# One more token chunk with the seven block products in the second FFN layer, and a new written-out order

## The chip, the cores and the metric

The kernel runs on one core of a Trainium2 chip. The time is device microseconds of one execution, the median of several. The profile is one further execution, recorded by the hardware profiler; its times count from its first instruction.

## The reference

For 8 batches of 576 positions with 8 heads of 64 the reference computes causal attention over a window of 64 positions, puts the heads side by side to a row of 512, takes a two-dimensional FFT of every batch (positions and features), keeps the real part, adds it to the input (`u`), normalises every row, and runs a feed-forward network on it:

```python
un = (u - mu) / np.sqrt(var + 1e-06)
ch = np.maximum(un @ w_ch1, 0.0) @ w_ch2      # 512 -> 2048 -> 512
return (u + ch).astype(np.float32)
```

## The kernel before, in words

**Work and tiles.** The 4608 rows are 36 tiles of 128 rows (`T`), worked on in attention, and 18 chunks of 256 rows (`c`), worked on in the FFN. A tile of attention is: loads of k, q and v (line 538), a split of k and q into two float16 parts and a DMA transpose of them (593), scores on TensorE (662), masking on VectorE (677), the exponential on ScalarE (685), a split of the result and two DMA transposes (715), the product with v (739), and normalising (758). Tiles 0 to 10 use float32 and TensorE transposes instead. When tiles 4 and 8 of a pair of batches are there, the FFT of a batch follows (1023, 1061), then for each tile a gather from DRAM, statistics and a split and transpose into the FFN's input (1135 to 1221).

**FFN.** TensorE works with three float16 products for each float32 product (`PASSES`). In `ffn` (chunks 1 to `SEVEN`-1; chunk 0 is float32) the first layer has 16 blocks of 12 matmuls with 256 columns (1419), ReLU into two parts on ScalarE (1428) and VectorE (1431), and the second layer has 16 blocks of 6 matmuls with 512 columns (1400). In `ffn7` (chunks from `SEVEN` on) the first layer is the same (1573); the second takes 8 steps `j`, each with seven block products of three matmuls with 256 columns (1548), as in Strassen's scheme, and so needs more work ahead of it: ReLU (1584), four sums of 128x128 (1589), the high part (510 or 506) and the low part (1597), on VectorE, ScalarE or GpSimd. The last chunk takes its last step by plain products (1560). The seven products also need sums of w2's blocks. `weight_sums` makes these once (VectorE lines 1493 to 1511, eight sets), into buffers that belong to attention until its last tile is done with them, so they can be made only at the end of attention and have to be there for the first `ffn7` chunk. Six chunks (12 to 17) use `ffn7`.

**Order.** Every step is an operation, entered by `plan.op` in a fixed sequence of calls and numbered in that sequence. `ORDER` lists these numbers: each engine works off its own in the order in which they stand there, so TensorE, VectorE, ScalarE, GpSimd and SyncE (which issues nearly all transfers) are five queues in order. `SECOND` holds the operations that go to the second of the two engines allowed to them. `plan.follow` checks the table and works out gaps, which serve for the warm-up matmuls (1759) in the first microseconds only; no time of it enters the program elsewhere. The tables were written by a planner that is not part of the kernel.

The numbers of `ORDER` can be turned back into operations by counting the calls for a given `SEVEN`; what the section on the change says of the two tables was read so.

Of the kernel before, what the change touches and what calls it, by code (L numbers as in the profile page):

```python
# [58 lines left out]
SEVEN = 12  # L59
# [339 lines left out]
def attn_fft_ffn_kernel(ctx: ExitStack, tc: tile.TileContext, q, k, v, w1, w2, gidx, dft_d, dft_s, mask, out):  # L399
# [1311 lines left out]
    for T in range(NTT):  # L1711
# [6 lines left out]
        if n in (4, 8):  # L1718
            base += FFT_AT + (FFT1 if T == 8 else 0)
            fft(2 * pb + n // 8, base)  # L1720
            for i, m in enumerate(range(0, 4) if n == 4 else range(4, 9)):
                args = NT * pb + m, base + NORM_AT + i + (EARLY if T == 4 and i > 1 else 0)
                if args[0] // 2 >= SEVEN + 4:
                    behind.setdefault(args[0] // 2, []).append(args)
# [66 lines left out]
```

## Time and profile before

| | us |
|---|---|
| median of 3 runs (lowest, highest) | 942.36 (940.58, 946.78) |
| the profiled execution: its own time | 945.16 |
| its span, first to last instruction | 943.4 |

The page of the profile gives the busy time of each engine, and then the span in 40 slices. PE is TensorE's matmuls, PEld its weight loads, DVE VectorE, ACT ScalarE, POOL GpSimd, SP SyncE. The end of a matmul is modelled, so that PE can be called busy where it does not work at its peak; the step from one block's start to the next one's is the safer reading.

### The profile page before, as it was taken

How to read it: one execution, taken by the hardware profiler on the slowest of the kernel's cores; microseconds unless marked ns; L12 is line 12 of the kernel's file. 1: busy time of each engine (PE TensorE's matmuls, PEld its weight loads, DVE VectorE, ACT ScalarE, POOL GpSimd, SP SyncE). 2: the span in 40 equal slices, each digit the busy share in tenths (PEclk: the TensorE clock that was granted, in tenths of full speed). 3: DMA queues.
4: the chain of work that ended last, by engine and by line, in shares of the span. 5: the costliest groups of instructions: out<-in, count | busy, mean ns of one | idle time of the engine just before them, and what ended most of it. 6: DMA issues, size and time to landing. Idle time of an engine off the chain costs nothing.

```text
span 943.4 us, 24809 instructions
## 1 busy us (share of the span) xinstructions
PE 924.2 (98%) x9717; PEld 703.2 (75%) x9717; DVE 705.3 (75%) x1982; ACT 435.1 (46%) x979; POOL 441.5 (47%) x823
## 2 busy tenths in 40 slices
PE   7799999999999999999999999999999999999998
PEld 6677777666766676666766676667779998888887
DVE  5898998887767866677658757888898965675664
ACT  6875777834555424445443543444334442422111
POOL 2653464744744555465746544655601454124012
PEclk9999999999999999999999999999999999999999
DMA  9997447999689969879979788785402032210100
GB/s 231 239 263 202 133 144 147 167 173 169 136 193 163 198 122 167 185 152 207 197 168 190 150 162 169 163 147 108 137 12 57 24 96 65 68 35 13 57 24 23
DMA packets 300230, 128.69 MB, mean 136 GB/s; under 512 B 277768, under 2 KB 278152, under 8 KB 300112
## 3 DMA queue, kind: packets, MB, share of 16 engines
q1 hardware_dynamic: 297248, 118.06, 59.6%
q0 software_dynamic: 2720, 8.92, 3.3%
q8 instruction: 76, 1.25, 0.6%
q14 instruction: 42, 0.34, 0.1%
q10 hardware_dynamic: 144, 0.13, 0.0%
HBM read 60.76 MB, written 19.94 MB: 86 GB/s over the span
## 4 chain that ended last, share of the span: by engine, by line
PE 83%; DMA 5%; DVE 4%; POOL 3%; SPq 2%; issue 2%; ACT 1%; POOLq 0%; DVEq 0%; ACTq 0%
PE ph L1419 22%; PE po L1400 22%; PE ph L1573 13%; PE po L1548 11%; PE pz L1061 3%; PE pg L1023 3%; PE pa L739 3%; PE psc L662 2%; DMA kn<-in_k 1%; POOL flex L516 1%; DMA ve<-va 1%; DMA qn<-in_q 1%; DMA pt<-flex 1%; SPq L1277 1%; PE py L850 1%
## 5 line engine op out<-in xcount | busy, mean ns | idle before, releaser
L1400 PE MATMUL po<-ws,hh 128*128 128x512 f16 (+1 forms) x1116 | 284.5, 391 | 0.5 <-issue 0.2
L1419 PE MATMUL ph<-room,ws 128*128 128x256 f16 x2112 | 256.1, 273 | 1.8 <-DVE hh L1431 1.8
L1419 PEld LDWEIGHTS <-ws 128*128 128x128 f16 x2112 | 205.3, 98 | 54.1 <-issue 2.8
L1400 PEld LDWEIGHTS <-hh 128*128 128x128 f16 x1056 | 101.1, 98 | 90.0 <-DVE hh L1431 0.7
L1573 PE MATMUL ph<-room,ws 128*128 128x256 f16 x1152 | 136.2, 273 | 0.0
L1573 PEld LDWEIGHTS <-ws 128*128 128x128 f16 x1152 | 112.6, 98 | 13.6
L1428 ACT ACTIVATE hh<-ph 128x512 f16<-128x512 f32 x88 | 52.3, 594 | 120.8 <-PE ph L1419 99.8
L685 ACT ACTIVATE pr<-pr,nm 128x128 f32<-128x128 f32 x288 | 91.2, 393 | 31.5 <-DVE nm L677 31.4
L1431 DVE SCALAR_TENSOR_TENSOR hh<-ph,hh 128x512 f16<-128x512 f32 x88 | 60.4, 686 | 36.6 <-ACT hh L1428 36.5
L1135 POOL DMA_INDIRECT mt<-md,gix x34 | 42.0, 1235 | 96.7 <-DVE mv L1163 81.5
L677 DVE CUSTOM_DVE_ANT_0 pr<-psc,mskb 128x128 f32<-128x128 f32 x288 | 65.0, 287 | 25.9 <-PE psc L662 19.7
L1584 ACT ACTIVATE hx<-ph 128x512 f32<-128x512 f32 x47 | 27.8, 595 | 113.3 <-PE ph L1573 103.7
L1589 DVE TENSOR_TENSOR hx<-hx 128x128 f32<-128x128 f32 x164 | 45.1, 318 | 37.8 <-ACT hx L1584 36.2
L1548 PEld LDWEIGHTS <-hh 128*128 128x128 f16 x658 | 64.4, 98 | 7.6
L1597 POOL TENSOR_TENSOR hl<-hx,hh 128x256 f16<-128x256 f32 (+1 forms) x40 | 28.0, 730 | 77.3 <-DVE hh L510 53.7
L516 POOL TENSOR_TENSOR up<-un,up 128x128 f16<-128x128 f32 x84 | 40.9, 516 | 46.3 <-ACT up L506 38.8
L516 POOL TENSOR_TENSOR flex<-pr,flex 128x128 f16<-128x128 f32 x92 | 42.5, 494 | 36.2 <-ACT flex L506 18.2
L1548 PE MATMUL po<-ws,hh 128*128 128x256 f16 x282 | 51.2, 273 | 0.0
L1597 DVE TENSOR_TENSOR hl<-hx,hh 128x896 f16<-128x896 f32 x37 | 40.4, 1097 | 7.8 <-ACT hh L506 6.5
L752 POOL TENSOR_TENSOR rc<-rc,mone 128x4 f32<-128x4 f32 x29 | 32.5, 1129 | 26.6 <-DVE rc L747 16.8
L739 PE MATMUL pa<-ve,pt 128*64 128x65 f16 (+1 forms) x776 | 37.0, 203 | 2.5 <-ACT ve L506 1.8
L1548 PE MATMUL po<-ws,hl 128*128 128x256 f16 x141 | 38.4, 273 | 0.0
(244 smaller groups left out, 1718.6 us busy)
## 6 DMA issues: line engine op xcount, KB each, us to landing
room<-in_moe_w_ch SPq DMA_DIRECT2D x20, 512.0 KB
flex<-in_moe_w_ch SPq DMA_DIRECT2D x12, 512.0 KB
ve<-va SPq DMA_DIRECT2D x47, 130.0 KB
flex<-in_v SPq DMA_DIRECT2D x22, 256.0 KB
xs<-xu SPq DMA_DIRECT2D x22, 256.0 KB
xv<-xs SPq DMA_DIRECT2D x22, 256.0 KB
out<-xv SPq DMA_DIRECT2D x21, 256.0 KB
md<-mp SPq DMA_DIRECT2D x24, 192.0 KB
```

Source lines behind the costliest of these rows:

```text
L516: eng.tensor_tensor(out=out[:, k : k + w], in0=in0[:, k : k + w], in1=in1[:, k : k + w], op=al)
L677: nc.vector.tensor_tensor_reduce(out=t["pr", g][:, hp], in0=t["ps", g][:, hp], in1=mskb[:, m : m + P], scale=-0.125, scalar=3.0e38, op0=AL ...
L685: nc.scalar.activation(pr, pr, AF.Exp, bias=t["nm", g][:, hp : hp + 1], scale=-1.0)
L739: nc.tensor.matmul(pa[sl, hp], pt[:, sl], v_, start=(x == 0), stop=(x == len(mm) - 1))
L1400: nc.tensor.matmul(t["po"][i], l_, r_, start=(f == 0 and x == 0), stop=(f == NKF - 1 and x == len(mm) - 1))
L1419: nc.tensor.matmul(ph, l_, r_, start=(x == 0), stop=(x == len(mm) - 1))
L1428: nc.scalar.activation(t["hh", j][:, 0], ph, AF.Relu)
L1431: nc.vector.scalar_tensor_tensor(out=hh[:, 1], in0=ph, scalar=0.0, in1=hh[:, 0], op0=ALU.max, op1=ALU.subtract)
L1548: nc.tensor.matmul(t["po", bk][:, x], t["h", j][a][:, slot], right(n, j, b_), start=(j == 0 and k == 0 and n in opens), stop=(j == seven - ...
L1573: nc.tensor.matmul(ph, l_, r_, start=(x == 0), stop=(x == len(mm) - 1))
L1589: eng.tensor_tensor(out=x[:, o], in0=x[:, p0], in1=x[:, p1], op=al)
L1597: eng.tensor_tensor(out=lo[:, a:b_], in0=x[:, a + 1 : b_ + 1], in1=hi[:, a:b_], op=ALU.subtract)
```

## The change

`SEVEN` goes from 12 to 11: chunk 11 moves from `ffn` to `ffn7`, and seven chunks take the seven block products. The bound from which norm operations are entered behind an `ffn7` chunk (`SEVEN + 4`) moves with it, which renumbers operations and changes no dependency. There are 3195 operations in place of 3178. `ORDER` and `SECOND` are replaced; the planner that wrote the new ones took every transfer to last 1.1 times as long.

```diff
-SEVEN = 12
+SEVEN = 11
...
 ORDER = [int(i) for i in """
-1 115 0 9 7 116 3 15 118 119 120 145 121 124 144 129 16 149 125 130 173 126 131 147 150 117 127 148 17 132 21 18 176 153
...
+690 1148 933 934 700 701 935 936 697 1177 1246 1178 1247 702 903 941 942 945 946 693 698 694 695 696 916 1183 955 705
...
 SECOND = {int(i) for i in """
-122 134 135 138 163 164 167 168 179 192 193 196 197 221 222 225 226 228 250 251 255 257 263 265 266 267 273 482 485 486
...
+123 128 134 135 138 139 152 161 163 164 167 168 181 192 193 197 221 222 226 228 250 251 254 255 257 265 267 269 270 273
...
```

The tables, turned back into operations, put these on the queues:

| stretch of TensorE's queue | before | after |
|---|---|---|
| from the v product of tile 10 to that of tile 35: first-layer, second-layer blocks of `ffn` and `ffn7` | 158, 159 | 146, 147 |
| from the scores of tile 35 to step j=6 of the first `ffn7` chunk: first-layer blocks, `ffn` second-layer blocks, groups of products | 41, 26, 8 | 37, 24, 8 |
| VectorE operations that the second stretch needs, counted from the last one that its first block needs | 132 | 128 |
| of them, sets of weight sums | 7 | 8 |
| the same, VectorE operations that stand in `ORDER` ahead of the scores of tile 35 though TensorE does not need them yet: us, at the median durations of the profile | 4 | 13 |
| whole program, operations on VectorE | 1023 | 1033 |

Among those that change their engine are the guards of attention's denominators (ScalarE 28, then 40).

## Rows read from the trace of the kernel before

**Rows 1.** Page, busy us (share) and instructions; clock and DMA share in 40 slices.

```profile
PE 924.2 (98%) x9717; PEld 703.2 (75%) x9717; DVE 705.3 (75%) x1982; ACT 435.1 (46%) x979; POOL 441.5 (47%) x823
...
PEclk9999999999999999999999999999999999999999
DMA  9997447999689969879979788785402032210100
```

**Rows 2.** Busy time by stretch: length, busy us (count) of each engine, clock, DMA.

```profile
0.00:86.00 86.00, 75.05 (x942) 58.83 (x944) 67.64 (x256) 61.92 (x156) 43.41 (x81) 1.00 0.95 237
86.00:158.00 72.00, 71.89 (x500) 51.21 (x497) 66.07 (x144) 50.96 (x105) 33.73 (x54) 1.00 0.51 147
158.00:283.50 125.50, 124.43 (x1442) 87.51 (x1436) 98.89 (x293) 71.60 (x165) 70.82 (x126) 1.00 0.87 167
283.50:393.00 109.50, 107.53 (x1310) 75.85 (x1303) 74.69 (x246) 48.75 (x118) 56.88 (x114) 1.00 0.89 166
393.00:478.00 85.00, 84.63 (x969) 59.95 (x968) 61.47 (x185) 40.51 (x101) 53.10 (x108) 1.00 0.93 186
478.00:653.20 175.20, 174.45 (x1984) 122.59 (x1976) 131.52 (x397) 74.71 (x179) 97.28 (x196) 1.00 0.80 156
624.50:737.40 112.90, 112.90 (x1073) 86.95 (x1073) 99.56 (x234) 41.76 (x83) 40.54 (x75) 1.00 0.36 82
737.40:908.00 170.60, 170.60 (x1579) 153.35 (x1578) 111.47 (x263) 52.66 (x95) 50.82 (x84) 1.00 0.18 49
```

**Rows 3.** Waits of PE, 190 to 660 us: total us, times, longest.

```profile
PE ph L1419 <- DVE hh L1431: 1.8, 3, 1.3
PE psc L662 <- issue: 1.3, 3, 0.6
PE pa L739 <- DMA ve<-va: 0.5, 1, 0.5
```

**Rows 4.** Chain that ended last, in order of time: start us, us, what.

```profile
621.96 2.59 PE po L1400 x12
...
712.22 2.29 PE po L1548 x21
...
755.94 3.93 PE ph L1573 x36
```

**Rows 5.** Timeline of PE at four marks: start us, us, instruction.

```profile
158.00 0.27 PE L739 MATMUL pa<-ve,pt 128*64 128x65 f32 x1
...
624.48 0.86 PE L662 MATMUL psc<-kst,qbd 64*64 64x128 f16 x48
...
653.24 0.22 PE L739 MATMUL pa<-ve,pt 128*64 128x65 f16 x1
...
704.53 0.38 PE L1548 MATMUL po<-ws,hh 128*128 128x256 f16 x2
```

**Rows 6.** Weight loads of TensorE: busy us, mean ns; idle before.

```profile
L1548 PEld LDWEIGHTS <-hh 128*128 128x128 f16 x658 | 64.4, 98 | 7.6
```

**Rows 7.** Page, costliest groups: busy us, mean ns; idle before, releaser.

```profile
L1428 ACT ACTIVATE hh<-ph 128x512 f16<-128x512 f32 x88 | 52.3, 594 | 120.8 <-PE ph L1419 99.8
L1431 DVE SCALAR_TENSOR_TENSOR hh<-ph,hh 128x512 f16<-128x512 f32 x88 | 60.4, 686 | 36.6 <-ACT hh L1428 36.5
L1584 ACT ACTIVATE hx<-ph 128x512 f32<-128x512 f32 x47 | 27.8, 595 | 113.3 <-PE ph L1573 103.7
L1589 DVE TENSOR_TENSOR hx<-hx 128x128 f32<-128x128 f32 x164 | 45.1, 318 | 37.8 <-ACT hx L1584 36.2
L1597 DVE TENSOR_TENSOR hl<-hx,hh 128x896 f16<-128x896 f32 x37 | 40.4, 1097 | 7.8 <-ACT hh L506 6.5
```

**Rows 8.** VectorE's costliest group between 624.5 and 737.4 us.

```profile
L1493 DVE TENSOR_TENSOR td<-td,ws 128x512 f32<-128x512 f32 x14 | 9.9, 707 | 0.5
```

274 rows, old and new, of tables (ORDER, SECOND) are left out of this document.

## The prediction

> **What bounds the kernel now.** [...] Then the stretches, cut at marks of TensorE's queue: tile 10's and tile 35's product with v at 158.0 and 653.2, the scores of tile 35 at 624.5, the first block product at 704.5 [rows 5]. Three phases show. Up to 86 us TensorE is idle for 11.0 us (86.00 less 75.05) at a DMA share of 0.95. From 158.0 to 653.2, 25 tiles of attention with FFN blocks between them, it is idle for 495.2 - 491.0 = 4.2 us (the four busy times are 124.43, 107.53, 84.63 and 174.45). From 624.5 to 908 it is never idle [rows 2]. The waits say who ended the few idle times: a VectorE step of the FFN, then TensorE's own issue, and one transfer, none over 1.3 us at a time [rows 3]. So the kernel is bound by TensorE's own work, with small losses in attention and a start bound by transfers. A cut of TensorE's work is worth its full length only where the other four queues follow the shorter schedule.
>
> **TensorE's work.** From the chain I take what a block lasts where nothing waits: 12 matmuls of 512 columns 2.59 us, so a second-layer block of `ffn` 1.295; 21 matmuls of a full step of `ffn7` 2.29; 36 matmuls of the first layer 3.93, so a block 1.31 [rows 4]. Chunk 11 gives up 16 x 1.295 = 20.7 us and takes 8 x 2.29 = 18.3 us. The first layer is the same. Term: **-2.4 us**, all on the path.
>
> [...]
>
> Chunk 11 will have 168 loads where it had 96. That they cost nothing rests on the 109 ns [rows 4] beside the 98 ns [rows 6]: the load goes on under the matmul before it.
>
> **The other engines' work for chunk 11.** VectorE drops 8 low parts at 686 ns (5.5 us) and takes most of 8 steps whose sums and low parts cost it (45.1 + 40.4)/47 = 1.8 us each, 14.6 us, and some high parts besides; ScalarE's ReLU stays (595 for 594 ns), and it takes some high parts [rows 7]. Counted over both tables, VectorE has some 11 us more in all. Most of that falls after 704 us, where VectorE is busy 111.5 of 170.6 us [rows 2]; the cover is that third of free time. The chunk's two output transfers stay two on SyncE's queue; its final additions on VectorE are within the 11 us; GpSimd gets seven steps of `ffn7` more and is busy 47% [rows 1]. What matters is when it falls.
>
> **VectorE at the end of attention.** The weight sums must now be there for chunk 11, and chunk 11's blocks no longer stand between attention and the first block product. Take the stretch from the scores of tile 35 to step 6 of the first `ffn7` chunk. Before, it lasts 112.9 us, VectorE busy 99.6 [rows 2] with the 132 operations of the table. After, TensorE has 4 first-layer and 2 second-layer blocks less there, 4 x 1.31 + 2 x 1.295 = 7.8 us: 105.1 us. VectorE needs 128 operations, but the mix is dearer: all of the eighth set of weight sums (its steps of 512 elements 707 ns each [rows 8]), and attention's steps that came earlier before. With the median duration of every kind, the sum over the operations rises by 4.6 us, to 104.2. The highest share that VectorE shows while TensorE goes on is 66.07/72.00 = 0.92 [rows 2]. At that pace 104.2 us take 113.5, 8.4 too many: the upper bound. Against it, the new table has 13 us of this work ahead of the scores of tile 35 rather than 4; with 9 us done early, 95.2/0.92 = 103.7 fits in 105.1: the lower bound, 0. I take **+2**, near the lower end, since the early work is in the table; not 0, since it must be earned in a stretch that is denser as well. Queued behind a late weight sum on VectorE stand the sums and low parts of chunk 11's steps, and TensorE's products wait for those.
>
> **Attention, denser.** Between tile 10 and tile 35 the new table has 24 FFN blocks fewer on TensorE (24 x 1.30 = 31.3 us), and one score and one FFT block more, some 2 us; so attention has 29 us less to do the same: 466 in place of 495.2. The new order thus asks more of the transfers. Their shares times lengths are 109 + 97 + 79 + 140 = 426 us of 16 engines' time [rows 2]; over 466 us that is a share of 0.91 for 0.86. For 85 us the trace shows 0.93 and at the start 0.95 [rows 2]. VectorE goes from 366.6/495.2 = 0.74 to 0.79. Lower bound: the 4.2 us of idle time go, since an order written for longer transfers puts TensorE's steps later behind them. Upper bound: no denser pace is possible, and TensorE waits the 29 us. I take **+1**, near the lower end, as 0.91 lies under what is shown.
>
> **The start.** The first steps are the same in another order, and TensorE reaches chunk 0 behind the same blocks. Nothing in the trace shows the new order; a fifth of the 11.0 us of idle time either way, -2 to +2, is my bound, and I take 0: about as many transfers and VectorE operations stand ahead of the marks. The guards that ScalarE takes over and the renumbered norms cost nothing: ScalarE is busy 46% [rows 1].
>
> **Sum.** -2.4 + 2 + 1 + 0 = +0.6 us. The profiled execution took 945.16 us (span 943.4); it would take 945.8. It lies 2.8 us above the median of 942.36, so the median to expect is 943.0.
>
> **Rivals.**
> *A: the order follows better, faster.* The idle time of attention goes (-4.2), VectorE is in time (0): 942.4 - 2.4 - 4.2 = 935.8 us. For it: transfers taken as 1.1 times as long leave room, and TensorE's waits there are short ones. Against it: the denser pace, and only one transfer among the waits [rows 3].
> *B: transfers become the bound of attention, slower.* Place: 158 to 653 us, scores and products with v waiting for transposes and copies. If the 16 engines can be kept busy to a share u on average, the stretch takes 426/u. At 0.89 that is 478.5, 12.5 us more than 466: 942.4 - 2.4 + 12.5 = 952.5; at 0.86 (the share before) 29 more, 969. It decides below u = 0.91, and costs over 1% below about 0.89. For it: 0.87 and 0.89 are what most of attention shows, with TensorE not idle for lack of them, so more has not been asked. Against it: 0.93 and 0.95 in the same trace.
> *C: each weight load takes its own time.* 72 loads more x 98 ns = 7.1 us, 943.0 + 7.1 = 950.1. The 109 ns speak against it. [...]
> *D: the change does not get its blocks into place.* TensorE's cut is eaten by late weight sums at the first block products, the full 8.4 us: 942.4 - 2.4 + 8.4 + 1 = 949.4.
>
> **How the numbers follow.** My forecast (no more than some us either way, 938 to 948) has 0.49, A 0.26, B 0.17, C 0.01, D 0.07. About 1% (9.4 us) is what a measurement of this kernel can tell from no change. Faster by that needs A and a shorter start together, 0.07. Slower by that is most of B and a little of D, 0.14. Within: 0.79. The predicted time is 943.0. The range goes from A with 1 us of start, 935, to B at u just under 0.89, 954, leaving about 0.1 on each side.
>
> **What would show it.** TensorE's step of 21 matmuls still 2.29 us, with 16 first-layer blocks and 8 steps of products more in `ffn7`: right on the first term. Tile 35's product with v some 25 to 33 us earlier in time (620 to 628), with a DMA share over 0.9 before it: the denser attention holds; if it comes after 630, B. TensorE idle between some 660 and 700 us with VectorE's weight sums or low parts as releasers: the second term, and its length D. Idle time of TensorE before 86 us near 11.0: the start. The prediction is wrong if the whole differs by over 1%, or if the loss in attention is other than 0 to 8 us.

## The result, and the profile after

The changed kernel takes 951.25 us (median of 20 runs, 946.94 to 955.03), the kernel before 943.98 on the same chips (20 runs, 940.58 to 949.09): 1.0071 times as long, 95% interval 1.0055 to 1.0087. (The ratios here and below are estimated over all runs; they are not the quotient of the two medians, 1.0077 here.) The profiled execution after took 949.88 us (span 948.1), 4.7 more than the one before; it lies 1.4 us below its median, where that of before lies 1.2 above its own. So the profiles show 4.7 of the 7.3 us.

The page after, which answers to [rows 1]: busy time, granted clock and DMA share.

```profile
PE 925.9 (98%) x9789; PEld 713.9 (75%) x9789; DVE 727.4 (77%) x1994; ACT 437.2 (46%) x992; POOL 448.0 (47%) x830
...
PEclk9999999999999999999999999999999999999999
DMA  9976464989799999999889987453202213120210
```

VectorE has 22 us more, twice the 11 that were counted: its instructions that exceed the median of their kind (same line, operation and tiles) by over 0.3 us exceed it by 21.8 us together, before by 8.2. The stretches do more. In this view of after (columns as in [rows 2]) the two short ones, 243 to 262 and 600 to 625, are those in which TensorE has holes.

```profile
0.00:86.00 86.00, 75.54 (x911) 60.12 (x913) 67.19 (x253) 59.01 (x152) 44.59 (x84) 0.96 0.92 232
86.00:158.00 72.00, 72.00 (x470) 51.70 (x466) 66.71 (x142) 51.75 (x108) 24.47 (x41) 1.00 0.54 153
158.00:243.00 85.00, 85.00 (x989) 58.51 (x990) 69.94 (x203) 51.15 (x115) 46.28 (x83) 1.00 0.91 166
243.00:262.00 19.00, 15.28 (x182) 11.13 (x172) 13.56 (x33) 7.64 (x23) 12.17 (x34) 0.91 0.73 130
262.00:600.00 338.00, 337.73 (x4131) 240.05 (x4126) 257.87 (x799) 164.23 (x403) 199.38 (x395) 1.00 0.96 185
600.00:625.00 25.00, 22.59 (x232) 15.88 (x230) 22.40 (x54) 9.51 (x22) 11.84 (x23) 1.00 0.39 89
625.00:640.00 15.00, 15.00 (x172) 11.81 (x171) 12.06 (x28) 3.41 (x11) 10.19 (x15) 1.00 0.46 109
640.00:710.00 70.00, 68.88 (x599) 55.58 (x597) 66.24 (x136) 26.60 (x50) 20.98 (x33) 1.00 0.22 55
710.00:908.00 198.00, 197.75 (x1827) 177.42 (x1825) 132.41 (x316) 56.88 (x101) 63.58 (x103) 1.00 0.20 48
```

From 262 to 600 us TensorE is idle for 0.3 us at a DMA share of 0.96: the denser attention runs. The waits of TensorE between 190 and 640 us, which answer to [rows 3], name two stops:

```profile
PE pg L1023 <- ACT hs L506: 3.4, 1, 3.4
PE ph L1419 <- DVE hh L1431: 2.4, 1, 2.4
PE pg L1023 <- DVE hs L516: 0.4, 1, 0.4
PE po L1400 <- DVE hh L1431: 0.3, 1, 0.3
```

A releaser is only the last link. The chain of waits at the first stop (start, us, what) shows what the released step itself had waited for:

```profile
245.96 1.03 POOL h L516 x3
...
247.01 4.86 DVE h L955
...
251.89 0.56 DVE h L516
252.46 0.56 DVE hs L516
...
253.06 1.06 PE pg L1023 x10
```

One VectorE instruction of 388 columns, a step of the FFT, lasts 4.86 us. The view of its line by form (minimum, median and maximum in ns) says that this is no property of the instruction; first before, then after:

```profile
L955 DVE SCALAR_TENSOR_TENSOR h<-h,yT x8: 552/601/1334, 52.0 to 697.0; 128x388 f32<-128x388 f32 x8
```

```profile
L955 DVE SCALAR_TENSOR_TENSOR h<-h,yT x8: 555/563/4846, 55.6 to 661.2; 128x388 f32<-128x388 f32 x8
```

Beside it GpSimd works off twelve instructions without a break, from 246.94 to 251.44 us; VectorE's instruction ends 0.42 us after the last of them. GpSimd's timeline of after:

```profile
245.61 1.37 POOL L516 TENSOR_TENSOR h<-yT 128x97 f32<-128x97 f32 x4
246.94 1.58 POOL L516 TENSOR_TENSOR flex<-qbd,flex 128x128 f16<-128x128 f32 x4
248.48 1.43 POOL L516 TENSOR_TENSOR f<-f,xe 128x97 f32<-128x97 f32 x4
249.87 1.57 POOL L516 TENSOR_TENSOR up<-un,up 128x128 f16<-128x128 f32 x4
```

The first of these lines releases VectorE, the other three are ready already. The same pair stands side by side once more, at 326 us, and there the two take turns: VectorE's step takes 0.77 us, and GpSimd's four instructions 2.67 in place of 1.58. VectorE and GpSimd, after:

```profile
326.42 0.77 DVE L955 SCALAR_TENSOR_TENSOR h<-h,yT 128x388 f32<-128x388 f32 x1 [0.88 <-POOL h L516]
```

```profile
326.34 2.67 POOL L516 TENSOR_TENSOR flex<-qn,flex 128x128 f16<-128x128 f32 x4
```

The second stop is of the same kind (chain of after): a low part of 512 columns that takes 0.69 us elsewhere, beside GpSimd's run from 607.78 to 612.18 us. The line at 615.08 is the hidden step that TensorE waits for, that is, the low part of the FFN's hidden values (line 1431). GpSimd's timeline of after stands behind it.

```profile
609.02 3.71 DVE flex L516
...
615.08 0.59 DVE hh L1431
```

```profile
607.78 1.54 POOL L516 TENSOR_TENSOR fs<-f,fs 128x97 f16<-128x97 f32 x4
609.29 1.57 POOL L516 TENSOR_TENSOR flex<-pr,flex 128x128 f16<-128x128 f32 x4
610.83 1.35 POOL L516 TENSOR_TENSOR fs<-f,fs 128x97 f16<-128x97 f32 x4
```

After the first stop the granted clock is at half (0.50) for at least the 2.6 us of this window, so the stop costs more than its length: the 24 first-layer matmuls from 254.12 us take 3.66 us in the chain, where [rows 4] has 3.93 for 36, that is 2.62 for 24.

```profile
253.00:255.60 2.60, 2.54 (x18) 2.08 (x19) 2.60 (x6) 2.20 (x7) 1.68 (x4) 0.50 0.30 69
```

The account over the span: the time from one TensorE block's start to the next one's, less what the block lasts where nothing waits (durations as in [rows 4]), summed by stretch.

| us lost by TensorE | before | after |
|---|---|---|
| 0 to 100 us | 21.7 | 23.1 |
| 100 to 250 | 2.9 | 1.9 |
| 250 to 300 (first stop) | 2.1 | 6.1 |
| 300 to 600 | 7.0 | 4.7 |
| 600 to 650 (second stop) | 0.5 | 3.6 |
| 650 to the end | 0.2 | 1.5 |
| work, against before | 0 | -2.4 |

The differences and the work add up to +4.1, and TensorE's first instruction comes 0.6 us later: the 4.7 us of the two profiles.

### The profile page after: what moved, and what is told of

Same layout as the page of the kernel before. It is cut to its first block, busy times and chain, and to the rows that moved or that the text cites. A ratio compares the mean times of both kernels' runs of the same rounds, so it can differ in the third digit from the quotient of the medians.

```text
span 948.1 us, 25025 instructions
## 1 busy us (share of the span) xinstructions
PE 925.9 (98%) x9789; PEld 713.9 (75%) x9789; DVE 727.4 (77%) x1994; ACT 437.2 (46%) x992; POOL 448.0 (47%) x830
## 4 chain that ended last, share of the span: by engine, by line
PE 82%; DVE 9%; POOL 4%; DMA 2%; issue 1%; ACT 1%; SPq 0%; POOLq 0%; DVEq 0%; ACTq 0%
PE ph L1419 23%; PE po L1400 22%; PE ph L1573 13%; PE po L1548 11%; PE pa L739 3%; PE psc L662 3%; PE pz L1061 3%; PE pg L1023 3%; DVE td L1493 1%; PE pp L696 1%; DVE hx L1589 1%; DMA dd<-in_dft_d 1%; DMA room<-up 1%; PE py L850 1%; DVE hl L1597 1%
## 5 line engine op out<-in xcount | busy, mean ns | idle before, releaser
L1400 PE MATMUL po<-ws,hh 128*128 128x512 f16 (+1 forms) x1020 | 261.5, 392 | 0.7 <-DVE hh L1431 0.7
L1428 ACT ACTIVATE hh<-ph 128x512 f16<-128x512 f32 x80 | 47.4, 593 | 94.5 <-PE ph L1419 70.3
L1589 DVE TENSOR_TENSOR hx<-hx 128x128 f32<-128x128 f32 x188 | 55.3, 335 | 34.8 <-ACT hx L1584 33.2
L1431 DVE SCALAR_TENSOR_TENSOR hh<-ph,hh 128x512 f16<-128x512 f32 x80 | 54.8, 686 | 28.1 <-ACT hh L1428 27.9
L1135 POOL DMA_INDIRECT mt<-md,gix x34 | 40.4, 1190 | 55.4 <-DVE mv L1163 34.3
L1597 POOL TENSOR_TENSOR hl<-hx,hh 128x256 f16<-128x256 f32 (+1 forms) x60 | 37.9, 661 | 58.0 <-DVE hh L510 25.7
L1176 POOL TENSOR_SCALAR rs<-mv 128x1 f32<-128x1 f32 x36 | 11.6, 323 | 109.1 <-ACT un L1170 105.9
L1597 DVE TENSOR_TENSOR hl<-hx,hh 128x896 f16<-128x896 f32 x40 | 43.8, 1098 | 23.4 <-ACT hh L506 21.7
L1548 PE MATMUL po<-ws,hh 128*128 128x256 f16 x330 | 60.0, 273 | 0.0
L516 POOL TENSOR_TENSOR y<-xu 128x128 f32<-128x128 f32 x80 | 42.7, 564 | 16.2 <-DVE xu L758 6.5
L1548 PE MATMUL po<-ws,hl 128*128 128x256 f16 x165 | 45.0, 273 | 0.7 <-DVE hl L1597 0.7
L516 POOL TENSOR_TENSOR flex<-pr,flex 128x128 f16<-128x128 f32 x68 | 32.3, 504 | 20.6 <-ACT flex L506 12.9
```

The source lines that it names most:

```text
L516: eng.tensor_tensor(out=out[:, k : k + w], in0=in0[:, k : k + w], in1=in1[:, k : k + w], op=al)
L1135: nc.gpsimd.indirect_dma_start(out=mts[T], out_offset=None, in_=mds[pb][0 : HR if n < 4 else 2 * HR], in_offset=bass.IndirectOffsetOnAxis( ...
L1400: nc.tensor.matmul(t["po"][i], l_, r_, start=(f == 0 and x == 0), stop=(f == NKF - 1 and x == len(mm) - 1))
L1428: nc.scalar.activation(t["hh", j][:, 0], ph, AF.Relu)
L1431: nc.vector.scalar_tensor_tensor(out=hh[:, 1], in0=ph, scalar=0.0, in1=hh[:, 0], op0=ALU.max, op1=ALU.subtract)
L1548: nc.tensor.matmul(t["po", bk][:, x], t["h", j][a][:, slot], right(n, j, b_), start=(j == 0 and k == 0 and n in opens), stop=(j == seven - ...
```

## The experiments

Theory 1 is that GpSimd's unbroken runs keep VectorE out at these two places. The rivals: an accident of one execution; too much VectorE work there; or the change of chunk 11 itself. Numbers in the diffs are those of the changed kernel's table; each line is the part of one engine's queue that changes.

**The same kernel again.** No edit.

> The changed kernel again, unaltered. Its profile had two long VectorE instructions that TensorE then waited for: a step of the FFT (line 955, 4.85 us where others of the form take 0.56) at 247 us and a low part (line 516, 3.71 us where others take 0.69) at 609 us, each beside a stretch in which GpSimd ran instruction after instruction without a break. Theory 1 (VectorE is kept out while GpSimd's run goes on, at the same places in every execution): both long instructions come again, within 1 us of the same places, and the time stays at 1.007 of before. Theory 2 (an accident of the one execution): they are gone or elsewhere, and the time varies by some 4 us with them. Theory 3 (VectorE has too much to do there): the waits are there, without an instruction of more than 1.5 us.

1.0073 of before (1.0044 to 1.0103); the profiled execution has 4.84 us for the step of line 955 at 246.0 us and 3.71 for the low part at 607.9. They are part of what this order does, not an accident.

**The run at 247 us.** 957 is the step of line 955, 956 what releases it; 1568 is q's low part, 948 f's total, 663 a norm's low part, 964 GpSimd's next FFT step.

```diff
-GpSimd:  956 1568 948 663 964
+GpSimd:  956 1568 964 663
-VectorE: 957 958 962
+VectorE: 957 958 948 962
-SECOND has 948
```

> The changed kernel with GpSimd's run at 247 us shortened: of the three operations behind the step that VectorE waits for, the total of f goes to VectorE and the low part of a norm goes behind the next FFT step of GpSimd; only the low part of q is left beside VectorE's step. Theory 1 (the run holds VectorE up): the step of line 955 takes at most 2.2 us, TensorE's 3.35 us wait at 250 us and the half clock after it go, and the kernel gains 3 to 5 us: 946 to 948, 1.003 of before. Theory 3 (too much VectorE work there): one operation more on VectorE, so the same wait or a longer one, 951 to 952, 1.007 to 1.008.

945.80 us, 1.0022 of before (1.0001 to 1.0043). The step takes 1.93 us, all four instructions that are left beside it, and the clock stays at 1.00 from 243 to 262 us, where TensorE's holes shrink from 3.7 to 1.1 us. VectorE has one operation more and the wait shrinks: it was not too much work. Shortening this one run of GpSimd gives back 5 of the 7 us. VectorE's timeline:

```profile
245.79 1.93 DVE L955 SCALAR_TENSOR_TENSOR h<-h,yT 128x388 f32<-128x388 f32 x1 [1.48 <-POOL h L516]
```

**The run at 609 us.** 2619 and 2620 are a weight sum, 2539 the low part that took 3.71 us, 1857 a hidden step.

```diff
-VectorE: 2619 2620 2539 ... 1857
+VectorE: 2619 2539 ... 1857 2620
```

> The changed kernel with VectorE's weight-sum operation of 2.6 us at 606 us moved behind the low part of a hidden step (line 1431) that TensorE waited for at 613 us, so that the low part of line 516 runs before GpSimd's run begins. Theory 1: that low part takes 0.7 us, TensorE's wait of 2.4 us goes, gain 2 to 3 us: 948 to 949, 1.004 to 1.005 of before. Theory 3 (too much VectorE work at the end of attention): what is moved is missed later, TensorE waits for weight sums before the first block product, gain under 1 us: 1.006 to 1.007.

950.77 us, 1.0077 (1.0050 to 1.0105): no gain that can be measured (the interval reaches some 2.6 us to either side), so I was wrong on its worth. The low part takes 0.69 us, but now another VectorE instruction meets GpSimd, the weight sum that was moved, and the next hidden step stands behind it. VectorE's timeline:

```profile
604.95 0.69 DVE L516 TENSOR_TENSOR flex<-pr,flex 128x512 f16<-128x512 f32 x1
...
611.31 2.01 DVE L1501 TENSOR_TENSOR td<-td,ws 128x256 f32<-128x256 f32 x1
...
615.48 0.68 DVE L1431 SCALAR_TENSOR_TENSOR hh<-ph,hh 128x512 f16<-128x512 f32 x1
```

TensorE waits twice, 0.7 and 0.6 us, in place of once for 2.4.

**Both.** The two edits together.

> Both of the edits at 247 and 609 us together. Theory 1: the gains add, 5 to 8 us: 943 to 946, 0.999 to 1.002 of before. Theory 3: no gain, 1.006 to 1.008. If the gain is that of one of them only, the other wait was no loss of its own.

945.53 us, 1.0020 (1.0000 to 1.0039). The gains do not add; the second edit is worth nothing that can be measured beside the first either.

**Moved further.** On top of the edit at 247 us, 1568 goes to VectorE ahead of 957, so that GpSimd has nothing left to do beside that step, and 2620 goes behind the second hidden step, 1853.

```diff
-GpSimd:  956 1568 964 663
+GpSimd:  956 964 663
-VectorE: 957 958 948 962
+VectorE: 1568 957 958 948 962
-VectorE: 2619 2620 2539 ... 1857 ... 1853
+VectorE: 2619 2539 ... 1857 ... 1853 2620
+SECOND has 1568
```

> The changed kernel with the edits at 247 us and, beyond them, the low part of q (the last operation of GpSimd beside VectorE's step) moved to VectorE ahead of that step, and the weight-sum operation at 606 us put behind the next two hidden steps rather than one. Theory 1 (GpSimd's unbroken runs hold VectorE up): the step of line 955 takes 0.6 us instead of the 1.93 that was left, TensorE's wait at 250 us goes altogether, and the hidden steps at 613 us come on time: 2 to 3 us less than with the first edit alone, 943 to 944, 1.000 to 1.001 of before. Rival (VectorE has no room left there): its added low part pushes the FFT steps back, TensorE waits at 250 us as long as with the first edit, 945 to 947.

942.88 us beside 946.40 for the kernel before on the same chip: 0.9974 of it (0.9955 to 0.9992), a little faster than both kernels. The two further moves were made together, so the time does not tell them apart. The line of the step by form, and the two stretches that had the stops (in the first VectorE has two operations more and is yet busy for less, and TensorE has 0.3 us of holes in place of 3.7; in the second none):

```profile
L955 DVE SCALAR_TENSOR_TENSOR h<-h,yT x8: 555/562/768, 53.4 to 653.1; 128x388 f32<-128x388 f32 x8
```

```profile
243.00:262.00 19.00, 18.71 (x230) 14.91 (x229) 12.79 (x35) 9.17 (x25) 13.91 (x32) 1.00 0.94 190
600.00:625.00 25.00, 25.00 (x272) 19.00 (x271) 20.45 (x49) 8.75 (x23) 13.91 (x24) 1.00 0.45 101
```

The account of lost time is 33.3 us (34.3 before, 40.8 in the changed kernel). With the stops out, the change is worth 2.5 us (0.8 to 4.2), beside the 2.4 of chunk 11's blocks.

**Six chunks in the new order.** The table with the edit at 247 us, chunk 11's operations replaced by those of a plain chunk.

```diff
-SEVEN = 11
+SEVEN = 12
-1:11.j, 7:11.j  (first layer, seven products, in the places of the new table)
+1:11, 2:11      (chunk 10's end and chunk 11 in the natural sequence, same places)
```

> The new order with the edit at 247 us, but with chunk 11 back in the plain second layer (six chunks with seven products): its blocks stand at the places of the chunk's blocks of the new table, chunk 10's end and chunk 11 in the sequence in which other plain chunks follow each other. It tells the order's part from the chunk's. If the chunk's change is worth its TensorE work (16 x 1.295 = 20.7 for 8 x 2.29 = 18.3), it takes 2.4 us more than the same order with seven chunks: 948, 1.005 of before; up to 1 us less than that if the wait for weight sums at 702 us goes with it. If the seventh chunk's extra VectorE work costs as much as TensorE saves, the two are equal: 946, 1.002. If the chunk's change is what made the kernel slower, this one is faster: 942 to 944.

956.89 us, 1.0100 (1.0068 to 1.0132), far more than any theory said, and inconclusive: the places that I gave to the blocks bring a wait of their own, 4.2 us at 705 us for an FFT step that stands on VectorE behind late hidden steps and weight sums, and a lower clock behind it (0.96 from 710 to 760 us).

```profile
PE pg L1022 <- DVE fs L515: 4.2, 1, 4.2
```

Beside that wait some 3 us are left of the 7.4 by which it is slower than the same order with seven chunks (1.0100 less 1.0022), and part of them is that clock. So nothing suggests that the chunk's change made the kernel slower, but what the chunk's change is worth is not measured here.

**VectorE and GpSimd alone.** A stretch after the last operation of the kernel before; everything is left in. SBUF is the memory in which the kernel's tiles lie.

```diff
+ for nm in (seven buffers, the first one twice): probe(nm, 8, "stt")
+ for n in (4, 12, 16): probe("q0", n, "stt")
+ for kind in ("tt", "one", "psum"): probe("q0", 8, kind)
+ for w in (64, 96, 112): probe("q0", 12, "stt", w)
```

> The kernel before, with a stretch added after its last operation in which VectorE and GpSimd alone work: 17 times GpSimd does four additions, and then 4 to 16 subtractions of 128 columns without a break (64, 96 or 112 columns in the last three), and VectorE, which waits for the four additions, does one operation of 388 columns. The first eight differ in the buffer that GpSimd reads; then the number of pieces differs, then the kind of VectorE's operation (plain addition, one input only, one input in PSUM), then the width. The time of the whole means nothing here. If VectorE is kept out by any unbroken run, its operation with two inputs in SBUF ends with the run each time (8 x 0.39 + 0.6 = 3.7 us) and that with one input, or one in PSUM, takes 0.6. If the two engines take turns, it takes 0.6 to 1.0 each time and GpSimd's pieces get longer. If it depends on the buffer or the moment, some of the eight take 0.8 and some 3.7.

The eight tests of seven buffers are alike, 0.77 us each. The test with 12 instructions takes turns, that with 16 does not; one input in SBUF takes 0.57 us, one of two in PSUM (where TensorE's results lie) 0.56, with GpSimd at full pace beside the latter. VectorE's timeline (in brackets what it had waited before):

```profile
985.11 0.77 DVE L1795 SCALAR_TENSOR_TENSOR flex<-flex 128x388 f32<-128x388 f32 x1 [2.40 <-POOL flex L516]
991.35 6.52 DVE L1795 SCALAR_TENSOR_TENSOR flex<-flex 128x388 f32<-128x388 f32 x1 [5.47 <-POOL flex L516]
...
1004.05 0.57 DVE L1801 TENSOR_SCALAR flex<-flex 128x388 f32<-128x388 f32 x1 [3.94 <-POOL flex L516]
1008.55 0.56 DVE L1803 SCALAR_TENSOR_TENSOR flex<-probe,flex 128x388 f32<-128x388 f32 x1 [3.94 <-POOL flex L516]
```

So there are two outcomes, turns (0.77 us) or a wait to the end of GpSimd's run (6.52), with the same instructions and the same buffers.

**A break in the run.** Two fills of one column on GpSimd, else the changed kernel.

```diff
+            if o.idx in (1568, 2544):
+                nc.gpsimd.memset(rest, 0.0)
```

> The changed kernel, order and engines untouched, with two instructions more: GpSimd fills one column of a small tile before the low part of q at 247 us and before the low part at 609 us, that is between the operation that releases VectorE and the next one of GpSimd's run, and in the middle of the run at 609 us. If VectorE loses because GpSimd's next instruction that reads SBUF always gets in ahead of it, a break of some 0.1 us lets it in: the step of line 955 falls from 4.85 to under 1 us, the low part at 609 us from 3.71 to under 2, and the kernel gains what the first edit at 247 us gave, 4 to 6 us: 1.001 to 1.003 of before. If the amount of work beside it is what counts, nothing changes: 1.007.

1.0065 (1.0040 to 1.0089): no gain. My picture of a race for the gap was wrong: the fill takes 0.10 us between 956 and 1568, VectorE's step starts at its end and still takes 4.89. The low part at 609 us takes 3.75.

```profile
246.35 0.10 POOL L1762 MEMSET rest<- 128x1 f32 x1
246.41 0.81 POOL L517 TENSOR_TENSOR flex<-qbd,flex 128x128 f16<-128x128 f32 x2
```

```profile
246.45 4.89 DVE L956 SCALAR_TENSOR_TENSOR h<-h,yT 128x388 f32<-128x388 f32 x1 [1.46 <-POOL h L517]
```

**Breaks everywhere.** The same fill before each of GpSimd's operations in the helper `both`, on the changed kernel and on the moved one.

> The changed kernel with the same one-column fill before each of GpSimd's two-input operations of line 516 (each of them four instructions), so that no run is longer than one operation. If breaks let VectorE in, no VectorE instruction of line 955 or 516 is held up by more than 1.6 us (one operation of GpSimd), and TensorE's waits at 250 and 613 us shrink; GpSimd does some 0.1 us more for each operation, which costs nothing at 47% busy: 1.000 to 1.003 of before. If the fills cost GpSimd's chains (splits ahead of transposes) more than the breaks give, 1.004 to 1.008.

> The kernel with the operations moved at 247 and 609 us, and the one-column fill before each of GpSimd's two-input operations. The remaining long ones (1.87 us at 494 us, 1.31 us at 47 us) would go: up to 1 us less than the moved one, 0.996 to 0.998 of before. If the fills shift GpSimd's chains, 0.998 to 1.003.

1.0074 (1.0046 to 1.0102) and 0.9981 (0.9963 to 1.0000), no better than without. The step of line 955 still takes 4.96 us in the first, and the low part at 497 us 1.93 in the second.

**What decides.** Two further stretches of the same test, 30 times at shifted moments, and 34 times with other lengths and places.

```diff
+ for k in range(30): nc.gpsimd.memset(lo16[:, 0:16 + 12 * k], 0.125); probe("q0", 8, "stt")
```

> The kernel before with an added stretch after its end, in which the same test is done 30 times: GpSimd does four additions that VectorE waits for and then eight subtractions of 128 columns without a break, VectorE one operation of 388 columns with two inputs in SBUF; ahead of each test a fill of another length shifts the moment at which it begins. The time of the whole means nothing. In the stretch measured first, one of 13 such tests held VectorE up for the whole run and the others took turns. If the moment decides, 1 to 6 of the 30 take 3.4 us or more and the rest 0.77; if the length of the run decides (only the one of 16 pieces was held up), none.

```diff
+ for n in (12, 16, 12, 16, 8, 16, 16, 13, 14, 15, 17, 18, 20, 24): probe("q0", n, "stt")
+ for w in range(1, 97, 5): late(10, w)
```

> The kernel before, with an added stretch after its end; the time of the whole means nothing. First the same test 14 times with 12, 16, 12, 16, 8, 16, 16, 13, 14, 15, 17, 18, 20 and 24 subtractions of GpSimd beside VectorE's operation of 388 columns; then 20 times with 10 subtractions, and a small VectorE operation with one input in PSUM (1 to 96 columns) ahead, so that the tested operation asks at 20 different places within GpSimd's instructions. If the length decides, the four of 16 (and perhaps the longer ones) are held up for the whole run, 6.5 us, and the others take 0.77. If the place within GpSimd's instruction decides, some neighbours of the 20 are held up for the rest of the run, about 3 us. If neither does, 0 to 2 of the 34 are held up, at no such places, and what decides stays open.

None of the 30 is held up, so the moment alone does not decide. Of the 34, seven are: three of the four with 16 instructions, those with 14, 17 and 20, and the first of the late ones. Neither length nor place explains it, but one thing goes with it: how long VectorE had gone without an operation that reads two operands from SBUF. Between these tests VectorE only waits, so the last timeline shows it in the brackets (not in its first line, ahead of which stand a fill and operations with an input in PSUM: there it is 7.6 us):

```profile
943.95 0.77 DVE L1795 SCALAR_TENSOR_TENSOR flex<-flex 128x388 f32<-128x388 f32 x1 [4.81 <-POOL flex L516]
950.19 6.52 DVE L1795 SCALAR_TENSOR_TENSOR flex<-flex 128x388 f32<-128x388 f32 x1 [5.47 <-POOL flex L516]
958.19 0.77 DVE L1795 SCALAR_TENSOR_TENSOR flex<-flex 128x388 f32<-128x388 f32 x1 [1.48 <-POOL flex L516]
964.43 6.52 DVE L1795 SCALAR_TENSOR_TENSOR flex<-flex 128x388 f32<-128x388 f32 x1 [5.47 <-POOL flex L516]
972.43 0.77 DVE L1795 SCALAR_TENSOR_TENSOR flex<-flex 128x388 f32<-128x388 f32 x1 [1.48 <-POOL flex L516]
977.13 0.77 DVE L1795 SCALAR_TENSOR_TENSOR flex<-flex 128x388 f32<-128x388 f32 x1 [3.94 <-POOL flex L516]
984.91 6.52 DVE L1795 SCALAR_TENSOR_TENSOR flex<-flex 128x388 f32<-128x388 f32 x1 [7.01 <-POOL flex L516]
```

Over the three stretches the eight held up came 5.47 us or more after the last such operation. Of the 71 with two operands in SBUF that took turns, 67 came 4.81 us or less after it; the other four, the first of each stretch (7.6 to 7.8 us) and one more (12.8), had VectorE operations of other kinds between. In these tests the wait is itself set by GpSimd's run before, so that it decides is not shown. The step at 247 us came 5.67 us after. But the low part at 609 us came straight behind another such operation, and others in the kernel, with operations of other kinds between, took turns after 5.5 to 7 us. What decides in the kernel stays open.

## Why the prediction was near and where it failed

The measured 951.25 us lie 8.25 above the 943.0 predicted and inside the range of 935 to 954. That is in part luck: the range reached so high for rival B, transfers as the bound, which did not come. What came, VectorE's steps held up by GpSimd, stands in no term and in no rival. On the profiles the sum is +4.7 us in place of +0.6.

**TensorE's work, -2.4: right.** 21 matmuls of `ffn7` still take 2.29 us after, 109 ns each, with 112 loads of `hh` more on line 1548 (770 for the 658 of [rows 6], 98 ns each as before), and 36 of the first layer 3.93 (chain of after):

```profile
711.13 3.93 PE ph L1573 x36
...
719.97 2.29 PE po L1548 x21
```

Rival C is out. The -2.4 of the account is worked out from these durations; no run measures it alone. The moved kernel's 2.5 us gain (0.8 to 4.2) is of that size.

**VectorE at the end of attention, +2: right in place, and in size by luck.** Between the prediction's own marks, from the scores of tile 35 (591.80 us after) to step 6 (699.03), the stretch takes 107.2 us where 105.1 + 2 were expected, and VectorE is busy 98.3 us of them, a share of 0.92. But TensorE is idle there for 2.8 us, and 2.4 of these are the second stop, a held-up instruction and not only the amount of VectorE's work. (The stop comes ahead of tile 35's product with v, so it lies in both of the prediction's stretches.) What the prediction described, block products that wait for a late low part, is 0.5 us at 699 us and 0.2 at 706; 0.4 more at 642 us stand behind a hidden step. Rival D did not come.

**Attention, denser, +1: this step failed.** Tile 35's product with v comes at 627.0, 26 us earlier, at a DMA share of 0.91 over the stretch, as was worked out, and of 0.96 from 262 to 600 us. So rival B is out and the pace asked for was possible. But the term's bounds looked at transfers only. The stretch between the marks takes 627.04 - 158.18 = 468.9 us, not 467: the old idle time went as rival A said (outside the two stops it fell from 4.2 to 0.3 us), and two new stops came, 4.0 and 3.1 us in the account. That the term is off by no more than 2 us is because these nearly cancel. The prediction had VectorE's busy share rise to 0.79 (0.78 came) and took GpSimd, busy 47%, as an engine with room; it never asked what runs beside VectorE's steps. That an engine has time says nothing on whom its operations keep waiting: beside twelve of GpSimd's instructions a step of 0.56 us took 4.86. The long instruction in the trace of before (1334 ns at 52 us on line 955) was the trace's own hint, and I did not look for it.

The order table could not have warned: in it 957 stands ahead of 1568, and `follow` lets the operations of VectorE and GpSimd that it calls `shared` run one at a time in the order of the table, so in its model VectorE goes first. On the chip GpSimd began 1568 at 246.94 us, 0.07 ahead.

**The start, 0: at the upper edge of its bounds.** In the account TensorE loses 1.4 us more up to 100 us and begins 0.6 later, +2.0 where -2 to +2 was allowed, at a clock of 0.96 up to 86 us. Tile 10's product with v yet comes at 158.18 for 158.00; in the ten profiles of the new order and its edits it begins between 156.0 and 159.6, so this varies from one execution to the next.

**The clock: not in the prediction.** Five profiles have the stop at 249 us at its full 3.3 to 3.6 us: the changed kernel twice, the edit at 609 us alone, and the two with fills and no moved operation. In all five the clock is lower from 243 to 262 us (a mean of 0.91 in four and 0.82 in one; in the profile after 0.50 from 253.0 to 255.6); in the other six, before among them, the clock is 1.00 there. Shorter stops go either way: behind the second one (2.4 to 2.5 us) it stays at 1.00 from 600 to 625 us in three profiles and is 0.93 in the one with breaks everywhere, and in the run with six chunks it is 0.93 behind 2.4 us.

The mean granted clock of the changed kernel's executions is 0.995 (median of 20); executions of before timed beside its second measurement have 1.000 (median of 25). Of 29 executions of the changed kernel, the 5 with a clock of 0.998 or more have a median of 947.3 us, the 17 with 0.995 or less one of 952.3. So a lower clock goes with differences of the size of the 2.6 us by which the medians lie further apart than the profiles. That the stop is what lowers the mean is shown in part only: in the profile after, the clock lacks 0.04 x 86 = 3.4 us before 86 us and 0.09 x 19 = 1.7 at the stop. With the edit at 247 us the median is 0.998.

## What to carry to other kernels

When an edit moves operations on an engine with time to spare, look for VectorE instructions with two operands in SBUF that start inside an unbroken run of such GpSimd instructions, as the two here that took 4.86 and 3.71 us did, above all on a chain that TensorE waits for: list a line by form and compare the maximum with the median. Keep the run away from the step (move it to VectorE ahead of the step, or behind the next dependent operation) rather than break it up (0.56 us for the step at 245 us in the moved kernel, 4.89 and 4.96 with fills); and price a stop of TensorE like the one of 3.3 to 3.6 us at 249 us with the clock as well, which was lower behind it (0.82 to 0.91 from 243 to 262 us) in all five profiles that have it.

## What the runs showed of the hardware that I had not expected

- VectorE instructions with two SBUF operands took up to the end of 4 to 20 GpSimd instructions beside them (1.93 us with 4, 8.06 with 20), though in 71 of the 79 tests with two such operands the two took turns (0.77 us for 0.56). With one operand in PSUM the one test took 0.56 us.
- The outcome is stable: at 247 us the step took 4.84 to 4.96 us in all five profiles that left its neighbours, with or without fills, and 1.92 to 1.93 in the three that left four instructions beside it.
- A fill of 0.10 us between GpSimd's instructions did not let VectorE in at 247 us: the step took 4.89 us with one fill, 4.96 with one before each operation.
